# Even and odd tokens interleaved on the partitions of a sliding-attention transformer layer

## The chip, the cores and the metric

The kernel runs on one core of one Trainium2 chip. Its engines work side by side: TensorE (PE, with PEld for the loading of its weights), VectorE (DVE), ScalarE (ACT), GpSimd (POOL), and SyncE (SP), which here issues nearly all transfers between DRAM and SBUF. The metric is the time of one execution in microseconds (us), as the median of several runs.

## What is computed

One layer over 2048 tokens with 640 channels, all in fp32: LayerNorm, attention with 32 heads of 20 channels, output projection and residual, LayerNorm, a SwiGLU network of width 1728 and residual. Attention is local and dilated: a token looks at itself and at the seven tokens 2, 4, ..., 14 before it, so even tokens never see odd ones.

```
h  = x + attention(layernorm(x)) @ wo
h2 = h + (silu(n @ w_gate) * (n @ w_up)) @ w_down      with n = layernorm(h)

idx    = pos[:, None] - 2 * arange(8)[None, :]          # window 8, dilation 2
logits = einsum("bhsd,bhswd->bhsw", q, k[idx]) * 20**-0.5, -1e9 where idx < 0
o      = einsum("bhsw,bhswd->bhsd", softmax(logits), v[idx])
```

## The kernel before

**Tiles.** The tokens come in four blocks of 512: 128 partitions with four tokens each (j = 0 to 3). Partitions 0 to 63 hold the even tokens of a block, 64 to 127 the odd ones; x and the output lie in DRAM in that order. The heads come in four groups of 8, 160 channels each. fp32 products are made of two parts of every operand, a high and a low one, in three passes. ACT makes the high part (a cast), DVE the low one (a subtraction): L667 and L668 for the weights of Q, K and V, L598 and L599 for turned columns, L1040 (low part) for the activations of the SwiGLU network.

**Buffers.** `fa` is one wide SBUF buffer that holds many things in ranges of its columns: the x tiles of a block (XR), the normalized x (XN), weights as they land, constants. `kv` holds loaded K and V, `st` the projected Q, K and V on their way out, `pq` the operands of attention, `h` the residual rows, `sha` and `shb` the columns that PE multiplies.

**Stages of a block and a group of heads.** LayerNorm 1: statistics by DVE (L513 and L514, a pair of statistics and their aggregate for one tile) or by ACT (L491 to L503). Transposition into columns by PE (L641) or, for some blocks, by DVE and DRAM: one DVE transpose of the block (L602), four stores to `ysc` (L604), one load of the columns (L608), then split by L598 and L599. Projection by PE (L696), eviction by ACT into `st` (L703), stores of K and V into the DRAM scratch `ksc` and `vsc` (L716) and of Q into `qsc` (L726, L729, L732). Attention loads Q (L747) and the windows of K and V (L752): a partition gets its four tokens and the seven before them, 11 x 160 = 1760 columns, for even and odd tokens by one transfer each over 64 partitions. Rows before the first token are zeros, stored once by L460. DVE multiplies Q with the K window (L767), sums (L773), ACT takes the exponentials, DVE multiplies with the V window (L808), adds up (L817) and turns the result (L824), which is stored to `osc` (L830). Then the output projection (L901; for the last block L1238), LayerNorm 2, gate and up (L989) and down (L1004, and L1158 and L1405 for two blocks in another scheme), and the output stores (L1423, L1499).

**Order.** Every operation is registered with its engine and with the ranges of columns that it reads and writes. A table of numbers, `ORDER`, written into the kernel, gives the order in which the operations of all engines are emitted; each engine runs its own in that order. SP's queue is one such list. Each transfer takes one of eight DMA semaphores in turn, so a transfer waits until the one eight before it has landed. Waits between engines are made when the program is built, from the accesses of the instructions as they are emitted, not from the ranges that were registered.

Of the kernel before, what the change touches and what calls it, by code (L numbers as in the profile page):

```python
# [21 lines left out]
SEQ = S // 2 + W - 1  # L22
# [305 lines left out]
def program(tc, x_in, wqkv_in, wo_in, ffn_in, ffl_in, const_in, out):  # L328
# [8 lines left out]
    with tc.tile_pool(name="sb", bufs=1) as sb, tc.tile_pool(  # L337
# [1270 lines left out]
```

## Time and profile before

| | |
|---|---|
| time, median of 3 runs | 843.38 us (842.36, 844.35, 843.38) |
| time of the profiled execution | 845.17 us |
| its span, first to last instruction | 843.4 us |
| granted TensorE clock | 1.00 |
| PE busy | 835.2 us (99%), 4049 matmuls |
| DVE busy | 744.5 us (88%), 934 instructions |
| ACT busy | 426.3 us (51%), 774 instructions |
| DMA packets | 89877, 174.88 MB, mean 207 GB/s |

Busy shares are means over the whole span. For a single stage one reads the busy time in that stretch and what ended the idle time in it. In rows of the trace, the two numbers in front are start and length in us; brackets at the end give the idle time before and what ended it. SPq rows are the issues of transfers by SP, not the transfers themselves.

### The profile page before, as it was taken

The numbers are of one execution on the slowest core, as the hardware profiler recorded it, in microseconds if no ns is written. First come the engines' busy times: TensorE is split into PE (matmuls) and PEld (weight loads), VectorE is DVE, ScalarE is ACT, GpSimd is POOL, SyncE is SP. The second block draws the span as 40 slices with busy tenths as digits, with TensorE's granted clock in tenths as the row PEclk, the third lists the DMA queues.
The fourth block names the chain that finished last, engine by engine and source line by source line (L and its number), as shares of the span: only waits on it lengthen the run. The fifth ranks groups of instructions, "written<-read, shape, count | busy, mean of one in ns | idle before, by whom it ended". The sixth has DMA issues, their size and how long they took to land. (4 is left out here: it accounts for less than half of the span.)

```text
span 843.4 us, 11052 instructions
## 1 busy us (share of the span) xinstructions
PE 835.2 (99%) x4049; PEld 717.4 (85%) x4049; DVE 744.5 (88%) x934; ACT 426.3 (51%) x774; POOL 3.4 (0%) x14
## 2 busy tenths in 40 slices
PE   8999999999999999999999999999999999999998
PEld 7888888889888888888888888888888888888998
DVE  6599999999999999999999999996797676576996
ACT  7966476244873343567345347554464323335451
POOL 0000000000000000000000000000000000000000
PEclk9999999999999999999999999999999999999999
DMA  7988977678788898877999989977522133475002
GB/s 250 261 214 239 271 177 195 186 209 234 175 246 250 270 272 289 229 237 234 299 288 304 261 242 270 257 281 274 167 78 100 57 113 100 156 256 222 0 33 93
DMA packets 89877, 174.88 MB, mean 207 GB/s; under 512 B 33744, under 2 KB 53200, under 8 KB 89056
## 3 DMA queue, kind: packets, MB, share of 16 engines
q1 hardware_dynamic: 88416, 173.53, 67.7%
q10 hardware_dynamic: 1408, 0.66, 0.3%
q8 instruction: 31, 0.51, 0.2%
q14 instruction: 22, 0.18, 0.1%
HBM read 126.04 MB, written 46.80 MB: 205 GB/s over the span
## 5 line engine op out<-in xcount | busy, mean ns | idle before, releaser
L989 PE MATMUL bank<-shb,rb 128*128 128x512 f32 x930 | 227.0, 390 | 1.4 <-DVE fa L1028 0.7
L989 PEld LDWEIGHTS bank<-shb,rb 128*128 128x128 f32 x930 | 173.2, 188 | 38.4 <-DVE fa L1028 2.1
L1004 PE MATMUL bank<-rb,acts 128*128 128x512 f32 x464 | 121.4, 391 | 0.0
L1004 PEld LDWEIGHTS bank<-rb,acts 128*128 128x128 f32 x464 | 86.4, 188 | 17.3
L767 DVE TENSOR_TENSOR pq<-kv,pq 128x2560 f32<-128x2560 f32 x32 | 90.2, 2819 | 3.2 <-DMA pq<-qsc 1.9
L817 DVE TENSOR_TENSOR pq<-pq 128x1280 f32<-128x1280 f32 (+2 forms) x96 | 89.6, 934 | 2.2
L808 DVE TENSOR_TENSOR pq<-kv,pq 128x2560 f32<-128x2560 f32 x32 | 90.3, 2821 | 1.3 <-DMA kv<-vsc 0.7
L773 DVE TENSOR_REDUCE pq<-pq 128x128 f32<-128x2560 f32 x32 | 90.1, 2814 | 0.2
L703 ACT ACTIVATE st<-bank,fa 128x480 f32<-128x480 f32 (+3 forms) x120 | 50.4, 475 | 43.2 <-PE bank L696 40.8
L901 PE MATMUL bank<-ra 128*128 128x320 f32 x360 | 55.9, 309 | 0.9 <-ACT fa L904 0.9
L901 PEld LDWEIGHTS bank<-ra 128*128 128x128 f32 x360 | 54.2, 188 | 2.7 <-ACT fa L904 1.3
L970 ACT CAST rb<-fa 128x1280 fp32r<-128x1280 f32 (+1 forms) x35 | 42.5, 1217 | 25.2 <-DMA fa<-in_ffn_dram 20.0
L696 PE MATMUL bank<-ra,sha 128*128 128x480 f32 (+2 forms) x240 | 53.6, 380 | 0.0
L696 PE MATMUL bank<-rb,sha 128*128 128x512 f32 (+1 forms) x240 | 52.6, 378 | 0.0
L696 PE MATMUL bank<-ra,shb 128*128 128x512 f32 (+1 forms) x240 | 52.0, 378 | 0.0
L696 PE MATMUL bank<-rb,shb 128*128 128x512 f32 (+1 forms) x230 | 50.8, 379 | 0.0
L696 PEld LDWEIGHTS bank<-ra,shb 128*128 128x128 f32 x240 | 45.0, 188 | 6.5
L696 PEld LDWEIGHTS bank<-rb,sha 128*128 128x128 f32 x240 | 44.9, 188 | 6.4
L696 PEld LDWEIGHTS bank<-ra,sha 128*128 128x128 f32 x240 | 44.5, 188 | 6.6 <-ACT sha L643 0.2
L696 PEld LDWEIGHTS bank<-rb,shb 128*128 128x128 f32 x230 | 42.9, 188 | 6.3
L965 DVE TENSOR_TENSOR rb<-fa,rb 128x640 fp32r<-128x640 f32 (+1 forms) x54 | 43.4, 818 | 1.3 <-DMA lsc<-rb 0.7
L1027 ACT ACTIVATE fa<-bank 128x512 f32<-128x512 f32 x34 | 20.3, 598 | 42.4 <-PE bank L989 38.4
(211 smaller groups left out, 1264.8 us busy)
## 6 DMA issues: line engine op xcount, KB each, us to landing
fa<-in_ffn_dram SPq DMA_DIRECT2D x35, 960.0 KB, 7.1
kv<-ksc SPq DMA_DIRECT2D x32, 440.0 KB, 6.7
kv<-vsc SPq DMA_DIRECT2D x32, 440.0 KB, 7.4
rb<-lsc SPq DMA_DIRECT2D x17, 640.0 KB, 5.8
lsc<-rb SPq DMA_DIRECT2D x13, 640.0 KB, 6.0
rb<-lsc SPq DMA_DIRECT2D x19, 320.0 KB, 6.8
ksc<-st SPq DMA_DIRECT2D x32, 160.0 KB, 3.7
vsc<-st SPq DMA_DIRECT2D x32, 160.0 KB, 3.1
```

Source lines behind the costliest of these rows:

```text
L696: T.matmul(banks[bk][:, 0:n], l, r_(wq(g, w, c) + shift, n), start=(p, c) == first_mm, stop=(p, c) == last_mm)
L703: P.add("ACT", act(m) + 0.06, lambda: A.activation(stage_t()[:, o : o + NJ * m].rearrange("p (t j c) -> p t j c", j=NJ, c=w)[:, :, j, :], ...
L767: P.add("DVE", dve(2560), lambda: V.tensor_tensor(pq(PROD, 2560).rearrange("p (j w c) -> p j w c", j=2, w=W), window(ko, 2 * jp), pq(qo + ...
L773: P.add("DVE", dve(2560), lambda: V.tensor_reduce(logits(lo)[:, :, 16 * jp : 16 * jp + 16].rearrange("p h n -> p n h"), pq(PROD, 2560).rea ...
L808: V.tensor_tensor(pq(PROD, 2560).rearrange("p (j n d) -> p j n d", j=2, d=DH), bass.AP(tensor=v.tensor, offset=v.offset, ap=[list(v.ap[0]) ...
L817: V.tensor_add(dst(v), v[:, :, 0:m, :], v[:, :, m : 2 * m, :])
L901: T.matmul(banks[bk][:, 0:320], l, r_(m, 320), start=p == 0 and c == 0, stop=p == 2 and c == NC - 1)
L965: low(640, lambda E, o=o: E.tensor_sub(ws(t, lo + o, 640)[p0:], fa[p0:, raw + o : raw + o + 640], ws(t, hi + o, 640)[p0:].bitcast(F32)), [ ...
L970: P.add("ACT", act(n), lambda: A.copy(ws(wt, gu, n), f(raw, n)), r=[rf(raw, n)], w=[rws(wt, gu, n)], prio=PR["fh"])
L989: T.matmul(banks[bk], ws(wt, gu + 1280 * w + wid * c + col, 128), x(a, c), start=p == 0 and c == 0, stop=p == 2 and c == NC - 1)
L1004: T.matmul(banks[k], l, m, start=first and p == 0, stop=stop and p == len(passes) - 1)
L1027: P.add("ACT", act(512), lambda: A.activation(f(so, 512), banks[5], AF.Silu), r=[pb(5)], w=[rf(so, 512)], prio=0, table="silu")
```

## The change

Partition p now holds a token of parity p mod 2: even and odd tokens alternate. A token's window then lies in its own partition and in the two of the same parity below it, two and four partitions away. The scratch of K and V is laid out by row of eight tokens, parity and 640 columns, so that one transfer of 128 partitions stores a block's K (or V), and two transfers over all 128 partitions load a window: one of 480 columns (three tokens of halo, L759) and one of 2 x 640 columns (the four tokens before and the partition's own four, L755). x and the output keep their order in DRAM, so each of their transfers is now two, one for the even and one for the odd partitions (`get`, L444, and `give`, L448). The zeros before the first token are four small transfers for K and four for V, and the constants for the mask come in two halves. The instructions of PE and DVE are the same in kind, shape and number; ACT has three table loads fewer. SP issues 550 transfers, not 543. The table `ORDER` is a new one of the same kind; the beginning of a row of each stands in the diff.

```diff
-SEQ = S // 2 + W - 1
+ROWS = S // 8 + 2
 ORDER = (
-    (3, 1, 1), (3, 0, 1), (2, 0, 1), (0, 0, 1), (1, 0, 1), (4, 2, 1), (4, 7, 1), ...
+    (3, 1, 1), (4, 2, 1), (3, 0, 1), (2, 0, 1), (2, 7, 1), (4, 7, 1), (1, 0, 1), ...
...
-        ksc = dr.tile([NG, 2, SEQ, GC], F32, name="ksc")
+        ksc = dr.tile([NG, ROWS, 2, NJ * GC], F32, name="ksc")
...
+        def get(t, o, n, x):
+            for a in range(2):
+                Q.dma_start(t[a:128:2, o : o + n], x[64 * a : 64 * a + 64])
+        def give(x, t, o, n):
+            for a in range(2):
+                Q.dma_start(x[64 * a : 64 * a + 64], t[a:128:2, o : o + n])
...
         def zero_halo(t):
-            Q.dma_start(
-                t[:, :, 0 : W - 1, :].rearrange("g a r c -> (g a) (r c)"),
-                pq_t()[0 : NG * 2, PROD : PROD + 1120],
+            for a in range(2):
+                Q.dma_start(t[:, 0, a, GC:], pq_t()[0:NG, PROD : PROD + 480])
+                Q.dma_start(t[:, 1, a, :], pq_t()[0:NG, PROD : PROD + 640])
...
         def load_x(b, js=None):
             if b:
-                ... Q.dma_start(f(XR, 2560), x_in[b].rearrange("p j c -> p (j c)")) ...
+                ... get(fa, XR, 2560, x_in[b].rearrange("p j c -> p (j c)")) ...
             for j in js:
-                ... Q.dma_start(f(XR + 640 * j, 640), x_in[0, :, j, :]) ...
+                ... get(fa, XR + 640 * j, 640, x_in[0, :, j, :]) ...
...
-            def put(par, dst, o):
+            def put(dst, o):
                 Q.dma_start(
-                    dst[g, par, 7 + 256 * b : 7 + 256 * b + 256, :].rearrange("(r j) c -> r (j c)", j=NJ),
-                    stage_t()[64 * par : 64 * par + 64, o : o + 640],
+                    dst[g, 64 * b + 2 : 64 * b + 66].rearrange("r a c -> (r a) c"),
+                    stage_t()[:, o : o + 640],
...
                     def ld(dst=dst, o=o, par=par):
-                        a = dst[g, par, 256 * b, :]
-                        Q.dma_start(kv_t()[64 * par : 64 * par + 64, o : o + 1760],
-                                    bass.AP(tensor=a.tensor, offset=a.offset, ap=[[640, 64], [1, 1760]]))
+                        if par:
+                            a = dst[g, 64 * b + 1, 0, :]
+                            Q.dma_start(kv_t()[:, o + 480 : o + 1760].rearrange("p (k c) -> p k c", k=2),
+                                        bass.AP(tensor=a.tensor, offset=a.offset, ap=[[640, 128], [1280, 2], [1, 640]]))
+                        else:
+                            a = dst[g, 64 * b, 0, GC:]
+                            Q.dma_start(kv_t()[:, o : o + 480], bass.AP(tensor=a.tensor, offset=a.offset, ap=[[640, 128], [1, 480]]))
...
-                P.add("SP", 0.45, lambda: Q.dma_start(out[2 + b, :, j, o : o + c], h_t()[:, lo : lo + c]), ...
+                P.add("SP", 0.9, lambda: give(out[2 + b, :, j, o : o + c], h_t(), lo, c), ...
```

What the table and the new transfers make of the order shows at three places. In the rows below, the first name is the line of the kernel, then the operation, the buffer written and read, the shape written, and what the instruction waits for: an engine or one of the eight DMA semaphores. Lines of the changed kernel are 3 to 6 higher than those of the kernel before.

*The start up to the first attention product, SP and ACT.* SP before:

```order
L587 DMA fa<-in_x_dram 128x640 x3
L660 DMA fa<-in_wqkv_dram 128x480 x3
L587 DMA fa<-in_x_dram 128x640
L660 DMA fa<-in_wqkv_dram 128x480
L1522 DMA fa<-in_const_dram 128x32 [waits DMAHW0_49]
```

SP of the change:

```order
L444 DMA fa<-in_x_dram 64x640 x2
L444 DMA fa<-in_x_dram 64x640 [waits DVE_49]
L444 DMA fa<-in_x_dram 64x640 x3
L663 DMA fa<-in_wqkv_dram 128x480 x2
L663 DMA fa<-in_wqkv_dram 128x480 [waits DMAHW0_49]
L663 DMA fa<-in_wqkv_dram 128x960 [waits DMAHW1_49]
```

The third transfer of x, which is the first half of the second tile, has a wait on VectorE that no transfer there had before, and the weights stand behind six transfers of x, not three.

Further on, Q, K and V of the first block are evicted by ACT (L703 before, L706 now) from four banks; `rb` is where weights of the next group go. ACT before:

```order
L703 ACTIVATE st<-bank_72,fa 128x3x160 [waits DVE_49,PE_49]
L703 ACTIVATE st<-bank_71,fa 128x3x160 [waits PE_49]
L703 ACTIVATE st<-bank_70,fa 128x3x160 [waits PE_49]
L703 ACTIVATE st<-bank_73,fa 128x3x160 [waits PE_49]
L491 ACTIVATE fa<-fa 128x640 [waits DMAHW5_49,DMAHW0_49]
```

ACT of the change:

```order
L706 ACTIVATE st<-bank_71,fa 128x3x160 [waits DVE_49,PE_49]
L670 CAST rb<-fa 128x512 [waits DMAHW1_49,DMAHW0_49]
L536 ACTIVATE fa<-fa 128x2 [waits Activation_49]
L670 CAST rb<-fa 128x512
L670 CAST rb<-fa 128x512 [waits DMAHW3_49,DMAHW2_49]
L670 CAST rb<-fa 128x512
L706 ACTIVATE st<-bank_70,fa 128x3x160 [waits PE_49]
L706 ACTIVATE st<-bank_72,fa 128x3x160 [waits DVE_49,PE_49]
L706 ACTIVATE st<-bank_73,fa 128x3x160 [waits PE_49]
```

SP of the change, behind the last of these evictions:

```order
L719 DMA ksc<-st 128x640 [waits DMAHW5_49,Activation_49]
L465 DMA ksc<-pq 4x480 [waits DMAHW6_49]
L466 DMA ksc<-pq 4x640 [waits DMAHW7_49]
L465 DMA ksc<-pq 4x480 [waits DMAHW0_49]
L466 DMA ksc<-pq 4x640 [waits DMAHW1_49]
L663 DMA fa<-in_wqkv_dram 128x2x448 [waits DMAHW2_49,DVE_49]
L731 DMA qsc<-st 128x640 [waits DMAHW3_49]
L719 DMA vsc<-st 128x640 [waits DMAHW4_49]
L759 DMA kv<-ksc 128x480 [waits DMAHW6_49,DMAHW5_49,DMAHW7_49,DMAHW1_49,DMAHW0_49]
L755 DMA kv<-ksc 128x2x640
L749 DMA pq<-qsc 128x640 [waits DMAHW3_49]
```

Four casts moved in between the evictions, and the zero transfers for K stand between the store of K and its load.

*The turned columns of the second block, SP and DVE.* SP before, from the load of the columns to that of the next block's x:

```order
L608 DMA fa<-ysc 128x5x512 [waits DMAHW6_49,DMAHW1_49,PE_49]
L729 DMA qsc<-st 128x640 [waits DMAHW7_49]
L830 DMA osc<-pq 32x5x64 [waits DMAHW0_49]
L732 DMA qsc<-st 512x1x32 [waits Activation_49]
L716 DMA ksc<-st 64x640 [waits DMAHW2_49,Activation_49]
L830 DMA osc<-pq 32x5x64 [waits DMAHW3_49,DVE_49]
L584 DMA fa<-in_x_dram 128x2560 [waits DMAHW4_49]
```

SP of the change:

```order
L607 DMA ysc<-fa 32x20x128 [waits DMAHW6_49,DVE_49]
L607 DMA ysc<-fa 32x20x128 [waits DMAHW7_49]
L607 DMA ysc<-fa 32x20x128 [waits DMAHW0_49]
L607 DMA ysc<-fa 32x20x128 [waits DMAHW1_49]
L836 DMA osc<-pq 32x5x64 [waits DMAHW2_49]
L836 DMA osc<-pq 32x5x64 [waits DMAHW3_49]
L611 DMA fa<-ysc 128x5x512 [waits DMAHW4_49,DMAHW6_49,DMAHW1_49,DMAHW7_49,DMAHW0_49,PE_49]
L444 DMA fa<-in_x_dram 64x2560 [waits DMAHW5_49,Activation_49]
L444 DMA fa<-in_x_dram 64x2560
```

DVE of the change, from the second V product after the transpose on:

```order
L814 TENSOR_TENSOR pq<-kv,pq 128x2560 [waits DVE_49]
L823 TENSOR_TENSOR pq<-pq 128x2x640 [waits DVE_49]
L823 TENSOR_TENSOR pq<-pq 128x2x320 [waits DVE_49]
L823 TENSOR_TENSOR pq<-pq 128x2x160 [waits DVE_49]
L830 STREAM_TRANSPOSE pq<-pq 128x2x5x32 [waits DMAHW5_49,DMAHW3_49,DVE_49]
L602 TENSOR_TENSOR sha<-fa,sha 128x4x128 [waits DMAHW5_49,DMAHW4_49,DMAHW6_49,PE_49,Activation_49]
L602 TENSOR_TENSOR sha<-fa,sha 128x4x128
```

The load of x moved up to stand right behind that of the columns and waits for ACT; the first subtraction of the columns (L602 now, L599 before) waits for three DMA semaphores, where it waited for one.

*PE around 559 us.* `bank7` takes the output projection of the last block (L1238 before, L1244 now), `acts` is the split activation. Before:

```order
L1238 MATMUL bank7_77<-ra_66 128x320 [waits DVE_49]
L1238 MATMUL bank7_77<-ra_66 128x320 x3
L1004 MATMUL bank3_73<-rb_67,acts_2094 128x512 x3
L1004 MATMUL bank4_74<-acts_2094,rb_67 128x512 x3
L1004 MATMUL bank2_72<-rb_67,acts_2094 128x512 x3
L1004 MATMUL bank4_74<-acts_2094,rb_67 128x512 [waits DVE_49]
```

Of the change:

```order
L1244 MATMUL bank7_77<-ra_66 128x320 x9
L1010 MATMUL bank3_73<-rb_67,acts_2076 128x512 x3
L1010 MATMUL bank1_71<-rb_67,acts_2076 128x512 x3
L1010 MATMUL bank4_74<-acts_2076,rb_67 128x512 x3
L1010 MATMUL bank0_70<-rb_67,acts_2076 128x512 x3
L1244 MATMUL bank7_77<-ra_66 128x320 [waits Activation_49]
L1244 MATMUL bank7_77<-ra_66 128x320 x8
L1010 MATMUL bank4_74<-acts_2076,rb_67 128x512 [waits DVE_49]
```

Nine more products of the output projection stand ahead of the wait for VectorE.

More of the change, by code (lines that the diff above doesn't have):

```diff
@@ L394, in program @@
         banks = [psp.tile([128, 512], F32, name=f"bank{i}") for i in range(8)]
-        ksc = dr.tile([NG, 2, SEQ, GC], F32, name="ksc")
-        vsc = dr.tile([NG, 2, SEQ, GC], F32, name="vsc")
+        ksc = dr.tile([NG, ROWS, 2, NJ * GC], F32, name="ksc")
+        vsc = dr.tile([NG, ROWS, 2, NJ * GC], F32, name="vsc")
         qsc = dr.tile([NB, NG, 128, NJ, GC], F32, name="qsc")
@@ L459, in zero_halo @@
         def zero_halo(t):
-            Q.dma_start(
-                t[:, :, 0 : W - 1, :].rearrange("g a r c -> (g a) (r c)"),
-                pq_t()[0 : NG * 2, PROD : PROD + 1120],
-            )
+            for a in range(2):
+                Q.dma_start(t[:, 0, a, GC:], pq_t()[0:NG, PROD : PROD + 480])
+                Q.dma_start(t[:, 1, a, :], pq_t()[0:NG, PROD : PROD + 640])
         for nm, t in (("K", ksc), ("V", vsc)):
@@ L583, in load_x @@
             if b:
-                P.add("SP", 0.65, lambda: Q.dma_start(f(XR, 2560), x_in[b].rearrange("p j c -> p (j c)")), w=[rf(XR, 2560)], prio=PR["x"], nbytes=nb(512, 2560))
+                P.add("SP", 1.0, lambda: get(fa, XR, 2560, x_in[b].rearrange("p j c -> p (j c)")), w=[rf(XR, 2560)], prio=PR["x"], nbytes=nb(512, 2560))
                 return
             for j in js:
-                P.add("SP", 0.45, lambda j=j: Q.dma_start(f(XR + 640 * j, 640), x_in[0, :, j, :]), w=[rf(XR + 640 * j, 640)], prio=0, nbytes=(1.3 if j else 1.1) * nb(128, 2560))
+                P.add("SP", 0.9, lambda j=j: get(fa, XR + 640 * j, 640, x_in[0, :, j, :]), w=[rf(XR + 640 * j, 640)], prio=0, nbytes=(1.3 if j else 1.1) * nb(128, 2560))
         def span(nm, lo, hi):
@@ L721, in qkv @@
             for nmd, dst, o in (("K", ksc, ko), ("V", vsc, ko + 640)):
-                for par in range(2):
-                    P.add("SP", 0.65, lambda par=par, dst=dst, o=o: put(par, dst, o), r=[("ab", o, o + 640)],
-                          w=[(f"{nmd}{g}{par}", 1000 + 256 * b, 1256 + 256 * b)], prio=PR["kvs"], nbytes=nb(64, 2560))
+                P.add("SP", 0.65, lambda dst=dst, o=o: put(dst, o), r=[("ab", o, o + 640)],
+                      w=[(f"{nmd}{g}{par}", 1000 + 256 * b, 1256 + 256 * b) for par in range(2)], prio=PR["kvs"], nbytes=nb(128, 2560))
                 if nmd == "K" and n == 448:
@@ L750, in ld @@
                     def ld(dst=dst, o=o, par=par):
-                        a = dst[g, par, 256 * b, :]
-                        Q.dma_start(kv_t()[64 * par : 64 * par + 64, o : o + 1760],
-                                    bass.AP(tensor=a.tensor, offset=a.offset, ap=[[640, 64], [1, 1760]]))
+                        if par:
[5 more added lines that the diff above has]
+                            Q.dma_start(kv_t()[:, o : o + 480], bass.AP(tensor=a.tensor, offset=a.offset, ap=[[640, 128], [1, 480]]))
                     lo_r = 0 if b == 0 else 1000 + 256 * (b - 1)
-                    P.add("SP", 0.45, ld, r=[(f"{nmd}{g}{par}", lo_r, 1000 + 256 * (b + 1))], w=[(f"fakv{par}", o, o + 1760)], prio=PR["atl"], nbytes=nb(64, 7040))
+                    P.add("SP", 0.45, ld, r=[(f"{nmd}{g}{q}", lo_r, 1000 + 256 * (b + 1)) for q in range(2)], w=[(f"fakv{par}", o, o + 1760)], prio=PR["atl"], nbytes=nb(128, 5120 if par else 1920))
             return b, g, n, ko, vo, qo, lo, mo
@@ L874, in wo @@
             if b:
-                P.add("SP", 0.6, lambda: Q.dma_start(h_t()[:, h0 : h0 + 2560], x_in[b].rearrange("p j c -> p (j c)")),
+                P.add("SP", 1.0, lambda: get(h_t(), h0, 2560, x_in[b].rearrange("p j c -> p (j c)")),
                       w=[("sha", h0, h0 + 2560)], prio=PR["old"], nbytes=nb(512, 2560))
@@ L910, in wo @@
                     xr = XR + 640 * (j % 2)
-                    P.add("SP", 0.45, lambda j=j, xr=xr: Q.dma_start(f(xr, 640), x_in[0, :, j, :]), w=[rf(xr, 640)], prio=PR["old"], nbytes=nb(128, 2560))
+                    P.add("SP", 0.9, lambda j=j, xr=xr: get(fa, xr, 640, x_in[0, :, j, :]), w=[rf(xr, 640)], prio=PR["old"], nbytes=nb(128, 2560))
                     P.add("DVE", dve(640), lambda lo=lo, hi=hi, j=j, xr=xr: V.tensor_add(h_t()[:, lo:hi], f(xr, 640), f(XN + 640 * j, 640)),
@@ L1212, in wo3 @@
             hr = lambda j, o=0, n=640: ("sha", 2560 + 640 * j + o, 2560 + 640 * j + o + n)
-            P.add("SP", 0.6, lambda: Q.dma_start(h_t()[:, 2560:5120], x_in[3].rearrange("p j c -> p (j c)")), w=[("sha", 2560, 5120)], prio=PR["old"], nbytes=nb(512, 2560))
+            P.add("SP", 1.0, lambda: get(h_t(), 2560, 2560, x_in[3].rearrange("p j c -> p (j c)")), w=[("sha", 2560, 5120)], prio=PR["old"], nbytes=nb(512, 2560))
             slot = lambda i: OT + 512 * i
@@ L1422, in store @@
                 lo = 2560 * b + 640 * j + o
-                P.add("SP", 0.45, lambda: Q.dma_start(out[2 + b, :, j, o : o + c], h_t()[:, lo : lo + c]), r=[("sha", lo, lo + c)], prio=3, nbytes=nb(128, 4 * c))
+                P.add("SP", 0.9, lambda: give(out[2 + b, :, j, o : o + c], h_t(), lo, c), r=[("sha", lo, lo + c)], prio=3, nbytes=nb(128, 4 * c))
             ps = range(m)
@@ L1498, in finish @@
                     lo, hi = hsl(b, j, o, e - o)
-                    P.add("SP", 0.45, lambda lo=lo, hi=hi, o=o, e=e, j=j: Q.dma_start(out[b, :, j, o:e], h_t()[:, lo:hi]), r=[("sha", lo, hi)], prio=3, nbytes=nb(128, 4 * (e - o)))
+                    P.add("SP", 0.9, lambda lo=lo, hi=hi, o=o, e=e, j=j: give(out[b, :, j, o:e], h_t(), lo, hi - lo), r=[("sha", lo, hi)], prio=3, nbytes=nb(128, 4 * (e - o)))
         def ln2_columns(b, prio):
@@ L1521, in program, with load_mask @@
         load_x(0, (3,))
-        P.add("SP", 0.45, lambda: Q.dma_start(f(MASK, 32), const_in[:, 0:32]), w=[rf(MASK, 32)], prio=6, nbytes=nb(128, 128))
+        def load_mask():
+            for a in range(2):
+                Q.dma_start(fa[a:128:2, MASK : MASK + 32], const_in[64 * a : 64 * a + 64, 0:32])
+        P.add("SP", 0.9, load_mask, w=[rf(MASK, 32)], prio=6, nbytes=nb(128, 128))
         ln1(0)
```

454 rows, old and new, of the table ORDER are left out of this document.

## The prediction

> **What bounds the kernel now.** I read the busy times first, then the waits of TensorE (PE), then busy time by stretch, then the groups of VectorE (DVE).
>
> The first line is part 1 of the page, the rest the waits of PE, with us in total, times, and the longest.
>
> ```profile
> PE 835.2 (99%) x4049; PEld 717.4 (85%) x4049; DVE 744.5 (88%) x934; ACT 426.3 (51%) x774; POOL 3.4 (0%) x14
> ```
> ```profile
> PE bank L568 <- POOL rb L1508: 1.9, 1, 1.9
> ...
> PE bank L1004 <- DVE acts L1040: 0.3, 1, 0.3
> ```
>
> PE looks like the whole story: busy for 99%, hardly a wait. But busy time is a mean over stages, so I cut the span at the first attention product (36.19) and at PE's last wait before a stretch without any (559.21). Columns: PE, PEld, DVE, ACT, POOL busy with counts, granted clock, DMA share, GB/s.
>
> ```profile
> 0.00:36.19 36.19, 33.83 (x154) 28.57 (x155) 18.73 (x45) 28.60 (x64) 1.17 (x7) 1.00 0.83 252
> 36.19:559.21 523.02, 520.40 (x2499) 446.17 (x2497) 511.30 (x518) 282.08 (x511) 0.73 (x2) 1.00 0.84 246
> 559.21:840.17 280.96, 280.96 (x1398) 242.62 (x1398) 214.02 (x372) 115.63 (x200) 1.51 (x5) 1.00 0.37 131
> ```
>
> In the middle DVE is busy for 511.30 of 523.02 us; what is left is 11.7 us over 518 instructions, 23 ns apiece, the step from one to the next. PE is as full only because the order gives it exactly what DVE releases. At 559.21 PE waits for a DVE subtraction (L1040), and everything DVE did is a queue ahead of that point. After it PE has 280.96 us without a gap, and DVE has slack (214.02). So the time is made of four parts: DVE's idle time in the head (36.19 − 18.73 = 17.46, a little of it steps), DVE's work up to L1040, PE's rest (280.96), and the tail, 843.4 − 840.17 = 3.2. DVE's and PE's instructions are the same in kind, shape and number after the change. So I look for idle time added to or taken from DVE before 559, PE work moved across that wait, and the tail.
>
> The groups of DVE that read K and V, with shapes kept apart: busy, mean ns of one | idle before them and what ended it. The last row has three shapes in one: a half, a quarter and an eighth of a product's columns.
>
> ```profile
> L808 DVE TENSOR_TENSOR pq<-kv,pq 128x2560 f32<-128x2560 f32 x32 | 90.3, 2821 | 1.3 <-DMA kv<-vsc 0.7
> L767 DVE TENSOR_TENSOR pq<-kv,pq 128x2560 f32<-128x2560 f32 x32 | 90.2, 2819 | 3.2 <-DMA pq<-qsc 1.9 <-DMA kv<-ksc 0.8 <-DMA osc<-pq 0.2
> L773 DVE TENSOR_REDUCE pq<-pq 128x128 f32<-128x2560 f32 x32 | 90.1, 2814 | 0.2
> ...
> L824 DVE STREAM_TRANSPOSE pq<-pq 128x320 f32<-128x320 f32 x32 | 16.3, 510 | 0.8
> ```
> ```profile
> L817 DVE TENSOR_TENSOR pq<-pq 128x1280 f32<-128x1280 f32 (+2 forms) x96 | 89.6, 934 | 2.2
> ```
>
> **The change part by part.** *K and V in one store and two full-width loads.* DMA issues: KB each, median us to landing.
>
> ```profile
> kv<-ksc SPq DMA_DIRECT2D x32, 440.0 KB, 6.7
> kv<-vsc SPq DMA_DIRECT2D x32, 440.0 KB, 7.4
> rb<-lsc SPq DMA_DIRECT2D x17, 640.0 KB, 5.8
> ```
>
> A load of 440 KB over 64 partitions takes 6.7 to 7.4, one of 640 KB over 128 takes 5.8, so the new loads should land earlier. But in all 64 products DVE waited 0.8 + 0.7 = 1.5 us for K and V: that is the most this can bring. It can bring nothing (the waits come from when a buffer comes free, not from the transfer). I take −0.5, as the loads are wider but their order behind other transfers is new.
>
> The Trainium skill ("SBUF — State Buffer", section "Door 1: The DMA port swizzle") says that partitions 0 to 63 reach 8 of 16 ports and all 128 reach 16. The three rows agree in direction (6.7 for fewer bytes, 5.8 for more). By that rule alone the whole 1.5 would go; the sum would be 1.0 lower.
>
> *x in halves, at the start.* The start of the trace of before:
>
> ```profile
> 0.80 1.35 SPq L587 DMA_DIRECT2D fa<-in_x_dram  x3
> 2.19 1.38 SPq L660 DMA_DIRECT2D fa<-in_wqkv_dram  x3
> 3.59 0.89 DVE L513 BATCH_NORM_STATS2 fa<-fa 128x6 f32<-128x320 f32 x2 [2.66 <-DMA fa<-in_x_dram]
> 3.61 0.43 SPq L587 DMA_DIRECT2D fa<-in_x_dram  x1
> ...
> 4.51 0.21 DVE L514 BATCH_NORM_AGGREGATE fa<-fa 128x2 f32<-128x12 f32 x1
> ...
> 6.88 0.89 DVE L513 BATCH_NORM_STATS2 fa<-fa 128x6 f32<-128x320 f32 x2 [1.57 <-DMA fa<-in_x_dram]
> ...
> 9.66 3.30 PE L696 MATMUL bank<-ra,sha 128*128 128x480 f32 x14
> ```
>
> Before, three x tiles go out between 0.80 and 2.15 and nothing holds them. In the order of the changed kernel the third transfer (first half of the second tile) waits for VectorE. Counting DVE's instructions, that is the aggregate of the first tile's statistics, ready at 4.51 + 0.21 = 4.7. It does not need those columns; the wait is made for a transfer that steps over every second partition of the same buffer. So four halves at 0.43 to 0.45 each leave from 4.7 to 6.5, and all that is queued behind them on SP is late: the weights at 6.5, not 2.19. The tile that was there at 6.88 has its second half asked for at 6.1; with some 2.5 to land (the three first tiles were there 3.59 − 0.80 = 2.8 after the first issue) it is there at 8.7, and the first projection, 9.66 − 6.88 = 2.8 behind it, starts at 11.5: **1.8 late**.
>
> The way from there to the first attention product:
>
> ```profile
> 23.29 1.22 ACT L703 ACTIVATE st<-bank,fa 128x480 f32<-128x480 f32 x2 [1.07 <-PE bank L696]
> ...
> 24.54 1.17 SPq L716 DMA_DIRECT2D ksc<-st  x2
> ...
> 26.87 0.69 DVE L668 TENSOR_TENSOR rb<-fa,rb 128x512 fp32r<-128x512 f32 x1 [4.34 <-DMA ksc<-st]
> ...
> 27.04 0.58 SPq L729 DMA_DIRECT2D qsc<-st  x1
> ...
> 30.13 0.33 SPq L747 DMA_DIRECT2D pq<-qsc  x1
> ...
> 36.19 2.83 DVE L767 TENSOR_TENSOR pq<-kv,pq 128x2560 f32<-128x2560 f32 x1 [1.86 <-DMA pq<-qsc]
> ```
> ```profile
> L667 ACT CAST rb<-fa 128x512 fp32r<-128x512 f32 x5 | 3.0, 614 | 0.0
> ```
> ```profile
> L668 DVE TENSOR_TENSOR rb<-fa,rb 128x448 fp32r<-128x448 f32 x5 | 2.9, 617 | 0.0
> ```
>
> ScalarE now has four casts of 0.614 (2.5 us) ahead of the last three evictions, so K is stored some 3.6 later (1.8, and 1.8 of the casts; the rest passes while PE ends). That is 28.2. Behind it on SP stand four small zero transfers and one of weights, ahead of the store of q: five issues at 0.33 to 0.45, 2.0 us, where before the second K store and two V stores stood, about 1.9. So the round trip of q keeps its length (24.54 to 36.19, 11.65) and the first product comes at 39.8, 3.6 late. DVE does three more 448-column subtractions first, 3 × 0.617 = 1.85 at most, 1.6 by the distance of their starts. So DVE's idle time grows by **+2.0**. From below: without the late start and the casts showing, the product comes at 36.2 with 1.6 more work done, −1.6. From above: +5, if the weights land late as well.
>
> *x of block 1 beside the turned columns.* Some LayerNorm output is turned by DVE, stored, loaded as columns, then split by ACT (L598) and DVE (L599).
>
> ```profile
> 72.50 2.85 DVE L602 STREAM_TRANSPOSE fa<-fa 128x2560 f32<-128x2560 f32 x1
> ...
> 88.13 0.39 SPq L608 DMA_DIRECT2D fa<-ysc  x1
> ...
> 96.06 0.62 ACT L598 CAST sha<-fa 128x512 fp32r<-128x512 f32 x1 [4.66 <-DMA fa<-ysc]
> ...
> 96.67 0.43 SPq L584 DMA_DIRECT2D fa<-in_x_dram  x1
> ...
> 101.96 0.68 DVE L599 TENSOR_TENSOR sha<-fa,sha 128x512 fp32r<-128x512 f32 x1
> ```
>
> Issues: all of the execution, then the one at 96.67 alone (last row):
>
> ```profile
> fa<-in_x_dram SPq DMA_DIRECT2D x3, 1280.0 KB, 9.5
> ...
> ysc<-fa SPq DMA_DIRECT2D x4, 320.0 KB, 5.1
> fa<-ysc SPq DMA_DIRECT2D x1, 1280.0 KB, 7.9
> ```
> ```profile
> fa<-in_x_dram SPq DMA_DIRECT2D x1, 1280.0 KB, 5.7
> ```
>
> Before, x of the next block is loaded after the columns, and neither engine waits for it. In the changed order its two halves stand right behind the load of the columns. The first waits for ACT's first cast, and the second cast and the first subtraction wait for both halves to land, again over other columns of the same buffer. Count from the end of the transpose. DVE then has to the subtraction one L773 (2.82), one L779 (2.81), two L814 with three sums and a transpose each (2 × (2.82 + 2.80 + 0.51) = 12.3), those groups being L767, L773, L808, L817 and L824 before, and eight small ones (1.8, estimate): 19.7. The columns take four stores in a row (four issues at 0.58, as the store of q above, and 5.1 to land: 7.4), the load 7.9, the cast 0.62, two halves (0.9 and 5.7): 22.5 (7.4 + 7.9 + 0.6 + 6.6). **+2.7** of DVE idle. From below 0 (the stores land sooner); from above 6.5, with 9.5 for x, the median of such loads, in place of 5.7.
>
> *Order at 559.* Nine 320-wide products of Wo that stood behind PE's wait for L1040 now stand ahead of it, and DVE's work ahead of L1040 is the same. The chain of waits has their price:
>
> ```profile
> 559.21 2.35 PE bank L1004 x9
> ...
> 561.99 1.31 PE bank L1238 x9
> ```
>
> PE's rest after the wait shrinks by **−1.3**. It brings nothing if the wait is no longer the one that decides.
>
> *Out in halves.* The last rows go out by two issues: one more at 0.43, less what a half lands sooner: **+0.35** (0 to 0.43). The x loads of the later blocks and the halo cost issues on SP alone; the cover is the distance at which they are asked for. ACT's three fewer table loads fall where it has 282.08 busy of 523.02: nothing.
>
> The Trainium skill ("DMA: Bandwidth & Descriptors", section "Rules for kernel authors") says not to split a transfer into two halves of the partitions, since both halves run on the same DMA engines and serialize. By that rule no half lands sooner than the whole, and the tail costs the full 0.43 in place of 0.35; no run here shows a split load of x yet.
>
> Sum: +2.0 + 2.7 − 0.5 − 1.3 + 0.35 = **+3.2**. The profiled execution took 845.17, 1.8 over its span and 1.8 over the median; it becomes 848.4. Against the median of 843.38 that is 846.6; I say **846.7**, with 844.5 to 849.5 as this case's own range.
>
> **The rivals.**
>
> A, *the head gains* (faster). The new order does three more subtractions ahead of the first product. If that product comes at about 36.2 to 36.5, DVE's idle time falls by 1.6. With columns in time that is −1.6 + 0 − 0.5 − 1.3 + 0.35 = −3.05: **840.3**. It decides when the first attention product starts before 37.8 (36.19 + 1.6): from there the head is a gain. For it: before, DVE stands 4.34 us in the head ahead of a subtraction of weights (the row at 26.87), which earlier weights would end sooner, and x tiles asked for in halves may land sooner. Against it: the wait at 4.7, and casts ahead of evictions.
>
> B, *late but covered* (within 0.2%). Head +2.0, columns in time: +0.55, **843.9**. For it: stores of 320 KB that follow each other may land sooner than 5.1, which was measured with others between them; 2.7 is small against a path of 22.5.
>
> C, *x in traffic*. The x load takes 9.5 beside K and V loads, and SP, which waits for the cast meanwhile, issues those late: +7.0, **850.4**. Two of three such loads were slower than the 5.7 one.
>
> **How the numbers follow.** Forecast 0.48, A 0.20, B 0.20, C 0.12. About 0.2% (1.7 us) is what a measurement of this kernel can tell from no change: faster is below 841.7, slower above 845.1. Faster: A nearly whole and a little of B, 0.21. Within: most of B, the low end of the forecast, 0.23. Slower: 0.56. The range takes in A and C: 840.5 to 850.5.
>
> **What would show it.** Right: the third x transfer issued at about 4.7, the first projection at 11 to 12, the first attention product at 39 to 41; near 105 a DVE wait of 1 to 5 us that ends with x, and an ACT cast that ends with x too; nine 320-wide products ahead of the last wait for L1046 (L1040 before). Wrong: a first product before 37.8, no DVE wait for x near 105, or PE with gaps that DVE does not explain; then my count of what the transfers wait for is off, or the K and V loads gave more than the 1.5 they can.

## The result, and the profile after

The changed kernel takes **853.89 us** (852.99 to 854.86, four runs), the kernel before 843.15 beside it: 1.0126 times as long (95% interval 1.0109 to 1.0144). Measured once more beside the experiments the ratio was 1.0127 (1.0098 to 1.0155). The prediction had the sign, slower, but its 846.7 is 7 us too low and the time lies above its range. The medians of two kernels further down leave out one run each that took far longer than all others (1197.69 us of the changed kernel, 1931.37 us of the one with K and V in halves).

The profiled execution of the changed kernel took 852.99, its span is 851.3; before, 845.17 and 843.4. The first is the fastest run of the changed kernel, the second is above all three runs of the kernel before, so the profiles show 7.9 us of the 10.7 between the medians. Busy times of the changed kernel:

```profile
PE 835.4 (98%) x4049; PEld 718.0 (84%) x4049; DVE 743.5 (87%) x934; ACT 420.9 (49%) x771; POOL 3.4 (0%) x14
```

The work is the same as before (PE 835.2, DVE 744.5). The waits of PE, in us in total, times, longest:

```profile
PE bank L644 <- ACT fa L499: 3.6, 1, 3.6
PE bank L571 <- POOL rb L1514: 1.9, 1, 1.9
PE bank L699 <- ACT st L706: 1.3, 1, 1.3
PE bank L644 <- DVE fa L518: 1.1, 1, 1.1
PE bank L556 <- DVE shb L560: 1.1, 2, 0.8
```

Before, PE waited for DVE's low part of the activations (L1004) and for other results between 288 and 559 us. None of that is left. All waits now lie early, as the cut of the span shows: to the first projection (14.37), to the first attention product (42.48), to the last early wait, to the end of PE. Columns as in the prediction's table of stretches.

```profile
0.00:14.37 14.37, 7.74 (x26) 5.65 (x27) 4.54 (x12) 5.05 (x10) 1.17 (x7) 0.81 0.55 169
14.37:42.48 28.11, 28.11 (x130) 24.09 (x131) 15.91 (x37) 25.03 (x57) 0.00 (x0) 0.98 0.84 264
42.48:149.77 107.29, 104.93 (x502) 90.73 (x502) 100.42 (x91) 59.80 (x140) 0.00 (x0) 1.00 0.66 216
149.77:844.47 694.70, 694.63 (x3393) 597.54 (x3392) 622.10 (x796) 330.98 (x565) 2.23 (x7) 1.00 0.60 203
```

From 149.77 on PE is busy for 694.63 of 694.70 us: **PE is the bound now**, not DVE. At the place where PE waited for L1040 before (L1046 now), DVE's result is there at 563.80 and PE comes for it 1.2 us later:

```profile
563.11 0.69 DVE L1046 TENSOR_TENSOR acts<-fa,acts 64x512 fp32r<-64x512 f32 x1
...
565.01 0.63 PE L1010 MATMUL bank<-acts,rb 128*128 128x512 f32 x2
```

Where the 7.9 us are: PE's idle time was 2.36 before 36.19 and 2.62 from there to 559.21, 4.98 in all; it is 6.63 + 2.36 + 0.07 = 9.06 now, 4.1 more. PE's busy time is 0.2 more. And from PE's end to the span's end it was 843.4 − 840.17 = 3.2, and is 851.3 − 844.47 = 6.8, 3.6 more. So three places: the start, a stretch around 112 us, and the tail.

*The start*, from the trace of the changed kernel:

```profile
0.80 6.95 SPq L444 DMA_DIRECT2D fa<-in_x_dram  x6
...
4.20 0.89 DVE L516 BATCH_NORM_STATS2 fa<-fa 128x6 f32<-128x320 f32 x2 [3.27 <-DMA fa<-in_x_dram]
...
7.79 2.96 SPq L663 DMA_DIRECT2D fa<-in_wqkv_dram  x6
...
10.36 0.89 DVE L516 BATCH_NORM_STATS2 fa<-fa 128x6 f32<-128x320 f32 x2 [4.44 <-DMA fa<-in_x_dram]
...
13.73 0.59 ACT L670 CAST ra<-fa 128x480 fp32r<-128x480 f32 x1 [1.50 <-DMA fa<-in_wqkv_dram]
...
14.37 1.17 PE L699 MATMUL bank<-ra,sha 128*128 128x480 f32 x2
...
42.48 2.83 DVE L773 TENSOR_TENSOR pq<-kv,pq 128x2560 f32<-128x2560 f32 x1
```

The six halves are issued over 6.95 us, with the wait for DVE's aggregate inside; the weights leave at 7.79 (2.19 before), the tile that DVE reads next, the third one issued, is there at 10.36 (6.88). The first projection starts at 14.37 (9.66), 4.7 late, right behind the cast of weights that had to land first. The first attention product comes at 42.48, 6.3 late.

*Around 112 us*, the columns, the x load and the engines behind it:

```profile
103.71 0.62 ACT L601 CAST sha<-fa 128x512 fp32r<-128x512 f32 x1 [0.29 <-DMA fa<-ysc]
104.36 1.18 SPq L444 DMA_DIRECT2D fa<-in_x_dram  x2
...
112.00 0.62 ACT L601 CAST sha<-fa 128x512 fp32r<-128x512 f32 x1 [7.67 <-DMA fa<-in_x_dram]
...
112.66 1.29 DVE L602 TENSOR_TENSOR sha<-fa,sha 128x512 fp32r<-128x512 f32 x2 [3.96 <-ACT sha L601]
...
113.79 1.50 PE L699 MATMUL bank<-rb,shb 128*128 128x448 f32 x6 [1.27 <-ACT st L706]
```

The x load leaves after the first cast, and the second cast waits 7.67 us for it. DVE loses 3.96. And ACT, which stands in that wait, has evictions behind it, for which PE waits 1.27. Some 35 us later PE waits another 1.1 for DVE (L560).

*The tail*, SP's issues of the last output stores and the last additions that they wait for. Before:

```profile
834.13 6.93 SPq L1423 DMA_DIRECT2D out_dram<-h  x7
...
840.21 0.49 DVE L1418 TENSOR_TENSOR h<-bank,h 128x320 f32<-128x320 f32 x1 [0.83 <-PE bank L1405]
```

Now:

```profile
837.67 11.34 SPq L448 DMA_DIRECT2D out_dram<-h  x18
...
842.30 0.49 DVE L1424 TENSOR_TENSOR h<-bank,h 128x320 f32<-128x320 f32 x1 [0.83 <-PE bank L1411]
...
843.18 0.49 DVE L1424 TENSOR_TENSOR h<-bank,h 128x320 f32<-128x320 f32 x1 [0.39 <-PE bank L1411]
...
844.50 0.49 DVE L1424 TENSOR_TENSOR h<-bank,h 128x320 f32<-128x320 f32 x1 [0.83 <-PE bank L1411]
```

Eighteen halves in 11.34 us, 0.63 from one to the next, the last of them issued 4 us after the last result. Before, seven whole stores stood in 6.93 us, with SP waiting for results between them, and the last issue ended 0.4 us after the last result.

And K and V, the groups that read them:

```profile
L814 DVE TENSOR_TENSOR pq<-kv,pq 128x2560 f32<-128x2560 f32 x32 | 90.3, 2821 | 0.6
L773 DVE TENSOR_TENSOR pq<-kv,pq 128x2560 f32<-128x2560 f32 x32 | 90.2, 2818 | 0.5
```

No transfer stands behind the idle time any more. The 1.5 us of waits are gone, as the prediction allowed.

### The profile page after: what moved, and what is told of

The parts are those of the page before. It is cut to its first block, busy times and chain, and to the rows that moved or that the text cites. A ratio compares the mean times of both kernels' runs of the same rounds, so it can differ in the third digit from the quotient of the medians.

```text
span 851.3 us, 11043 instructions
## 1 busy us (share of the span) xinstructions
PE 835.4 (98%) x4049; PEld 718.0 (84%) x4049; DVE 743.5 (87%) x934; ACT 420.9 (49%) x771; POOL 3.4 (0%) x14
## 4 chain that ended last, share of the span: by engine, by line
PE 88%; DVE 4%; DMA 3%; ACT 2%; SPq 1%; issue 1%; DVEq 0%; ACTq 0%
PE bank L995 29%; PE bank L699 16%; PE bank L1010 15%; PE bank L1164 13%; PE bank L907 6%; PE bank L1411 6%; PE bank L1244 2%; DMA fa<-in_x_dram 1%; DVE pq L773 1%; PE bank L556 1%; DMA fa<-ysc 1%; DVE pq L823 1%; DVE pq L814 1%; DMA ysc<-fa 1%; DMA fa<-in_wqkv_dram 1%
## 5 line engine op out<-in xcount | busy, mean ns | idle before, releaser
L706 ACT ACTIVATE st<-bank,fa 128x480 f32<-128x480 f32 (+3 forms) x120 | 50.7, 474 | 50.0 <-PE bank L699 48.6
L1024 ACT CAST acts<-fa 128x512 fp32r<-128x512 f32 x36 | 22.3, 621 | 42.1 <-DVE fa L1034 39.6
```

The costliest lines, as they stand in the source:

```text
L706: P.add("ACT", act(m) + 0.06, lambda: A.activation(stage_t()[:, o : o + NJ * m].rearrange("p (t j c) -> p t j c", j=NJ, c=w)[:, :, j, :], ...
```

## The experiments

Two theories. **Theory 1**: the halves of x and of the output cost the time, by waits that come with them and by their issues; K, V and the new order do no harm. **Theory 2**: the new order, or K and V in wide transfers, costs it. Most kernels below keep x and the output in DRAM in the interleaved order, so that each transfer can be whole or in halves while the table of the order stays the changed one:

```diff
-    x = a(A_x.reshape(NB, 64, NJ, 2, D).transpose(0, 3, 1, 2, 4).reshape(NB, 128, NJ, D))
+    x = a(A_x.reshape(NB, 64, NJ, 2, D).transpose(0, 1, 3, 2, 4).reshape(NB, 128, NJ, D))
...
-                Q.dma_start(t[a:128:2, o : o + n], x[64 * a : 64 * a + 64])
+                Q.dma_start(t[a:128:2, o : o + n], x[a:128:2])
```

Ratios are to the kernel before on the same chip. Ratios of four or five runs are known to about 0.15 to 0.3%, so the parts are also read from the profiles.

**Everything whole.** All x, output and mask transfers over 128 partitions.

```diff
-                P.add("SP", 0.9, lambda j=j: get(fa, XR + 640 * j, 640, x_in[0, :, j, :]), ...
+                P.add("SP", 0.9, lambda j=j: Q.dma_start(f(XR + 640 * j, 640), x_in[0, :, j, :]), ...
...
-                P.add("SP", 0.9, lambda: give(out[2 + b, :, j, o : o + c], h_t(), lo, c), ...
+                P.add("SP", 0.9, lambda: Q.dma_start(out[2 + b, :, j, o : o + c], h_t()[:, lo : lo + c]), ...
```

The other uses of `get` and `give`, and the mask, are changed in the same way.

> The changed kernel with x and the output kept in DRAM in the interleaved order, so that every transfer of x, of the output and of the mask is one over 128 partitions. K and V, and the table of the order, are as changed. Theory 1 (the loss comes from waits that the transfers over every second partition bring, plus slow output issues): first projection near 10 us, no wait for x near 112, tail 3.2 us; the 5.3 us at the start, 3.1 us between 112 and 149 and 3.6 us in the tail come back: about 842. Theory 2 (the loss is the new order and K and V in wide transfers): it stays above 850.

Measured: 840.84, ratio 0.9979 (0.9965 to 0.9993). Theory 2 falls: with the same order and the same K and V, the kernel is 0.2% faster than the one before. Measured again with the kernels compared further down:

> The kernel with everything whole once more. If its gain is real: 0.2% below the kernel before again, 0.9965 to 0.9993. If the first measurement was luck: within 0.1% of it.

840.53, ratio 0.9964 (0.9949 to 0.9979). Its waits of PE:

```profile
PE bank L571 <- POOL rb L1514: 1.9, 1, 1.9
PE bank L995 <- ACT fa L1033: 0.9, 2, 0.6
PE bank L644 <- DVE sha L647: 0.3, 1, 0.3
```

3.1 us, against 4.98 us of idle time before. No kernel of the study is faster. Its first attention product shows what the new order does without the halves:

```profile
38.11 2.81 DVE L773 TENSOR_TENSOR pq<-kv,pq 128x2560 f32<-128x2560 f32 x1
```

That is 1.9 later than before (36.19), and DVE is idle for 17.85 us up to there (17.46 before). The other 4.4 of the 6.3 come with the halves.

**One place at a time.** The output stores whole (the second edit above, at both uses of `give`), the start whole (the four x tiles of the first block), the x loads of the later blocks whole (those for LayerNorm 1):

> The changed kernel with DRAM in the interleaved order, x still in halves over every second partition, only the output stores whole. Both theories: nothing but the tail moves; if the tail of 6.9 us is the queue of output issues on SP (18 at 0.63 us), it falls to about 3.3 and the time to about 850.3. If the tail is the landing of the last rows, it stays at 853.9.

> The changed kernel with only the four x tiles of the first block whole, the rest in halves. Theory 1: first projection near 10 us, 4 us earlier; TensorE keeps its clock there; TensorE is the bound from 149 us on, so most of 5.3 us comes back unless VectorE takes over: 848 to 850. If the start is covered later by other slack: no change, 853.9.

> The changed kernel with DRAM in the interleaved order and only the x loads of blocks 1 to 3 for LayerNorm 1 whole, the start and the output in halves. Theory (TensorE is the bound from about 149 us on, so each loss before that counts in full): no wait for x near 112, the 3.1 us between 112 and 149 come back, 853.9 - 3.1 = 850.8. Rival (VectorE is the bound further on and is late from the start anyway): less than 1 us comes back.

Measured: output whole 850.46, ratio 1.0103 (1.0087 to 1.0118). Start whole 846.95, ratio 1.0061 (1.0046 to 1.0076). Later blocks whole 851.43, ratio 1.0112 (1.0097 to 1.0128). Against 1.0126 these are 0.23, 0.65 and 0.14% of 843, 1.9, 5.5 and 1.2 us. They add up to 8.6 of the 12.4 us between the changed kernel and everything whole. What is missing is about the size of the intervals, so the sum does not tell whether a fourth place matters (the x loads for the residual and the mask stay in halves in all three). The DRAM order alone does not move the start: with the output whole and x in halves the first projection comes at 14.26, as in the changed kernel.

In the profiles each does what it should. Output whole, the last issues of SP:

```profile
837.96 7.69 SPq L1429 DMA_DIRECT2D out_dram<-h  x9
...
844.80 0.49 DVE L1424 TENSOR_TENSOR h<-bank,h 128x320 f32<-128x320 f32 x1 [0.83 <-PE bank L1411]
```

The last store leaves right behind the last addition; the span ends at 848.2, 2.9 us behind it, where the changed kernel needs 6.3 (851.3 − 844.99). Start whole:

```profile
0.80 1.34 SPq L590 DMA_DIRECT2D fa<-in_x_dram  x3
2.18 2.98 SPq L663 DMA_DIRECT2D fa<-in_wqkv_dram  x6
...
8.86 2.40 PE L699 MATMUL bank<-ra,sha 128*128 128x480 f32 x10
```

The first projection at 8.86, 5.5 us earlier than in halves. And later blocks whole:

```profile
104.55 1.14 ACT L601 CAST sha<-fa 128x512 fp32r<-128x512 f32 x2 [0.40 <-DMA fa<-ysc]
...
109.27 1.25 DVE L602 TENSOR_TENSOR sha<-fa,sha 128x512 fp32r<-128x512 f32 x2
```

The casts follow each other and DVE does not wait: the wait at 112 belongs to the strided halves, not to the order, in which the load of x stands where it stood.

**The tail alone, on one chip.** All loads of x whole, the output alone in halves, beside the changed kernel and everything whole:

> The changed kernel itself once more, beside the two kernels that follow, so that the parts are compared on one chip. All theories: 1.2 to 1.3% over the kernel before.

> The changed kernel with DRAM in the interleaved order, all loads of x and the mask whole, the output alone in halves. If the tail is the queue of 0.6 us issues: TensorE's part is that of the kernel with everything whole, the tail 6.9 in place of 3.4 us, so 3.4 us (0.4%) above that kernel, about 0.2% over the kernel before. If most of the loss sat in the output stores: near the changed kernel.

Measured on the same chip: changed 853.82, x whole 843.90 (ratio 1.0010, 0.9996 to 1.0025), everything whole 840.53. So of 13.3 us the x loads hold **9.9** and the output stores **3.4**, as expected. In the kernel with x whole the tail is again a row of halves, 18 issues in 11.33 us:

```profile
828.55 11.33 SPq L448 DMA_DIRECT2D out_dram<-h  x18
```

**Is it the wait, or the number of transfers?** The 5.5 us of the start can come from the wait for DVE inside SP's queue or from six issues in place of three. Two kernels take this wait of SP away and leave the six issues. In the first the halves are partitions 0 to 63 and 64 to 127:

```diff
-                Q.dma_start(t[a:128:2, o : o + n], x[a:128:2])
+                Q.dma_start(t[64 * a : 64 * a + 64, o : o + n], x[64 * a : 64 * a + 64])
...
-                Q.dma_start(x[a:128:2], t[a:128:2, o : o + n])
+                Q.dma_start(x[64 * a : 64 * a + 64], t[64 * a : 64 * a + 64, o : o + n])
```

> The changed kernel with x and the output in two transfers each, but of partitions 0 to 63 and 64 to 127 in place of every second one. Theory 1a (the waits cost it): the start and the stretch at 112 come back, only the tail stays: 853.9 - 5.3 - 3.1 = 845.5. Theory 1b (the number of transfers and their slower issue cost it): the start stays late by most of its 5 us, 850 or more.

In the second the first three x tiles are emitted ahead of all else (the table of the order begins with them, nothing else moves). The wait then falls on DVE:

```diff
 ORDER = (
-    (3, 1, 1), (4, 2, 1), (3, 0, 1), (2, 0, 1), (2, 7, 1), (4, 7, 1), ...
+    (4, 2, 1), (4, 7, 1), (4, 4, 1), (3, 1, 1), (3, 0, 1), (2, 0, 1), (2, 7, 1), ...
```

> The changed kernel with DRAM in the interleaved order, all in halves, and the first three x tiles emitted ahead of the first statistics, SP's own order as it is. So SP no longer waits for VectorE after the second half; the wait turns up on VectorE, whose first aggregate now waits for all six halves. If SP's wait is what makes the start late: the weights leave at 4.6 us, not 7.8, TensorE's first projections come 2 to 2.5 us sooner, 1.3% over the kernel before falls to 1.0%. If only the number and the price of the halves count: no change at all.

Measured: halves of neighbours 852.75, ratio 1.0116 (1.0087 to 1.0146); issued first 850.46, ratio 1.0084 (1.0056 to 1.0111), 3.4 us below the 853.82 of the changed kernel on the same chip. The starts of the two, neighbours first:

```profile
0.80 3.79 SPq L444 DMA_DIRECT2D fa<-in_x_dram  x6
...
4.62 2.96 SPq L663 DMA_DIRECT2D fa<-in_wqkv_dram  x6
...
11.24 1.22 PE L699 MATMUL bank<-ra,sha 128*128 128x480 f32 x3 [0.84 <-ACT ra L670]
```
```profile
4.62 2.96 SPq L663 DMA_DIRECT2D fa<-in_wqkv_dram  x6
...
7.48 0.21 DVE L517 BATCH_NORM_AGGREGATE fa<-fa 128x2 f32<-128x12 f32 x1 [2.46 <-DMA fa<-in_x_dram]
...
11.68 0.77 PE L699 MATMUL bank<-ra,sha 128*128 128x480 f32 x1
```

Without the wait the weights leave at 4.62 in both, and the first projection comes at 11.24 and 11.68, not at 14.37. With whole tiles it is 8.86. So of the 5.5 us by which the first projection is late, about **2.7 to 3.1 are the wait** and **2.4 to 2.8 the halves themselves**: six issues take 3.8 us where three take 1.34, and weights queue behind them. In all four kernels the first projection starts 6.6 to 7.1 us after the first weights leave (at 2.18, 4.62, 4.62 and 7.79). The upper 2.8 is not the halves alone: in the second kernel the false wait has only moved (DVE's aggregate waits 2.46 for tiles that it does not read). My expectation for the neighbours, 845.5, was wrong. In its profile the wait at 112 is gone, as expected, but other waits come in its place, the largest behind a load of attention results that took 13.26 us (467.49 to 480.75):

```profile
PE bank L907 <- ACT fa L910: 4.2, 1, 4.2
```

Whether loads over 64 neighbouring partitions hold up what is behind them, or whether that one load was late by chance, is open: one profile doesn't tell, and this kernel's runs spread widely (849.94 to 855.56).

**The clock.** In the start of the changed kernel the granted clock falls. In stretches of 5 us (columns as above):

```profile
5.00:10.00 5.00, 1.97 (x10) 1.20 (x8) 0.84 (x3) 1.36 (x4) 0.00 (x0) 0.88 0.58 169
10.00:15.00 5.00, 3.28 (x12) 2.52 (x13) 3.46 (x8) 2.84 (x6) 0.00 (x0) 0.50 0.89 301
```

To see whether that costs time of its own, 14 more warming matmuls were put where PE waits 3.6 us:

```diff
-                    warm(1, 512, [("b5", 0, 0.25)])
+                    warm(15, 512, [("b5", 0, 0.25)])
```

> The changed kernel with DRAM in the interleaved order, halves as they are, and 14 more warming matmuls (3.2 us, their result is not used) in the 3.6 us in which TensorE waits for the second x tile. If the fall of the granted clock to 0.5 between 10 and 15 us costs time of its own: the clock stays near 1, the transposes at 12 us and the first projections run at full pace, 1.0 to 1.6 us come back, about 852.5. If the late x and weights alone set the start: no change, 853.9.

Measured: 855.08, ratio 1.0154 (1.0139 to 1.0170), not faster than the changed kernel. The stretch from 10 to 15 now has a clock of 0.96, but the first projection starts at 14.77, since it waits for the cast of late weights, and behind that wait the clock falls after all:

```profile
14.77 1.17 PE L699 MATMUL bank<-ra,sha 128*128 128x480 f32 x2 [2.02 <-ACT ra L670]
```
```profile
15.00:20.00 5.00, 5.00 (x17) 4.26 (x18) 4.82 (x9) 4.59 (x12) 0.00 (x0) 0.70 0.64 214
```

From 15 to 20 the clock is 0.70 here and 0.94 in the changed kernel. So the fall was moved, not taken away, and this kernel does not show what it costs. That the slow clock did not set the first projection is seen in the changed kernel itself: the cast that it needs ends at 14.32, and it starts at 14.37. Behind it the clock is still 0.50 up to 15 and 0.70 from 15 to 16, which makes about 0.6 us of PE's work (an estimate: 0.63 × 0.50 + 1.00 × 0.30). What else made the kernel with more warming slower is open.

**The nine products.** Everything whole, and the nine products of Wo behind the wait again, as before the change (PE's instructions in their order, not code):

```diff
 L1010 MATMUL bank_70<-rb,acts 128x512 x3
-L1244 MATMUL bank_77<-ra 128x320 x9
 L1010 MATMUL bank_74<-acts,rb 128x512 x2
 L1010 MATMUL bank_72<-rb,acts 128x512 x2
 L1010 MATMUL bank_73<-rb,acts 128x512 x2
+L1244 MATMUL bank_77<-ra 128x320 x9
```

> The kernel with everything whole (840.84) with nine of the 320-wide output projection matmuls put back behind TensorE's wait for the low part near 557 us, as they stood before the change. If VectorE sets the time of that wait, as the prediction had it: TensorE waits 1.3 us longer there and the time is 842.2. If TensorE is the bound there in this kernel, its wait being 0.2 us: between 840.8 and 842.2, at least no more than 0.5 us slower.

Measured: 841.07, ratio 0.9980 (0.9968 to 0.9991), against 0.9979 with them ahead. No difference. PE around the place:

```profile
554.58 0.72 PE L1010 MATMUL bank<-acts,rb 128*128 128x512 f32 x2
555.15 1.09 PE L1010 MATMUL bank<-rb,acts 128*128 128x512 f32 x4
556.07 1.49 PE L1244 MATMUL bank<-ra 128*128 128x320 f32 x9
```

PE runs through without a listed wait, its matmul that waits for DVE among them (at 554.58; DVE's subtraction ends at 554.53). The 1.3 us of the prediction do not exist in this kernel.

**The width of K and V.** Everything whole, but each load of K and V in two of 64 partitions:

```diff
-                            Q.dma_start(kv_t()[:, o : o + 480], bass.AP(tensor=a.tensor, offset=a.offset, ap=[[640, 128], [1, 480]]))
+                            for h in range(2):
+                                Q.dma_start(kv_t()[64 * h : 64 * h + 64, o : o + 480],
+                                            bass.AP(tensor=a.tensor, offset=a.offset + 40960 * h, ap=[[640, 64], [1, 480]]))
...
```

> The kernel with everything whole (840.84) with each load of K and V in two transfers of 64 partitions, 128 loads more. If the width of the K and V loads is worth something, waits of VectorE for K and V come back, up to the 1.5 us of the kernel before or more: 841.5 to 843. If these loads are hidden: 840.8, no waits for kv.

Measured: 842.62, ratio 1.0012 (1.0002 to 1.0022), against 0.9979 for everything whole: 2.8 us by the ratios. By the medians it is 1.6 us above the 841.07 of the kernel with the products put back, which ran on the same chip. But DVE waits only 0.4 us for V in its profile. PE's waits of the middle are for ACT and DVE:

```profile
PE bank L998 <- ACT fa L1036: 0.8, 2, 0.5
PE bank L998 <- DVE fa L1037: 0.6, 1, 0.6
```

So the split costs something, though not at the products that read K and V. Loads of 64 partitions and 64 more issues on SP (not 128, as the expectation has it) come together here, and which of them it is stays open.

## Why the prediction was wrong, point by point

- **What failed, in short.** The sum of +3.2 met 7.9 in the profiles and 10.7 between the medians. Two of its terms were mis-sized: the output in halves (+0.35, measured 3.4) and the late start (1.8, measured 4.4). A third, the order at 559 (−1.3), does not exist, since it rested on DVE setting the time there.
- **The frame: DVE's work up to 559 us, then PE's rest.** Its first part came out near, with luck. DVE's subtraction at the wait starts at 563.11 and started at 558.46, 4.65 earlier; the first three terms gave 4.2. But DVE lost 4.6 in the start and 3.96 at 112, not 2.0 and 2.7, and then won some back in waits that are gone, 1.5 of it for K and V. The step from there to PE's end failed. PE lost time of its own: its idle time up to 149.77 is 8.99, where it had 2.36, while the 2.62 us that it waited for DVE and others later are gone. It came to the place 1.2 us after DVE's result and runs from 149.77 to its end without a wait, so the loss is read from PE. Even before, this frame was one of two readings: PE was busy for 520.40 of the 523.02 us in the middle and waited about 1 us of them for DVE.
- **The start, +2.0.** Right in mechanism: the third transfer waits for DVE's first aggregate, weights queue behind it, casts stand ahead of evictions. The term was mis-sized. I had issues of 0.43 to 0.45 for halves and weights from 6.5; the halves took 0.63 each (3.78 for six without a wait), the first tile landed later and the aggregate with it, and the weights left at 7.79. The first projection came at 14.37, not 11.5, the first product at 42.48, not 39.8. DVE's idle time up to there is 42.48 − 4.54 − 15.91 = 22.0, 4.6 more than before. The part for the casts and the three subtractions was right: +1.8 and −1.6 stand against 1.9 and DVE idle 0.4 longer with everything whole. Of the late first projection about half was not the wait but twice the issues. One reading was wrong too: 2.8 after the first issue the first tile alone was there; the other two were read at 4.53 and 6.88, though they had been issued by 2.15.
- **x beside the columns, +2.7.** The best step. The place, the cast that waits, the subtraction that waits are as predicted; the halves landed 7.6 after the first issue (6.6 predicted) and DVE lost 3.96, inside the bounds of 0 to 6.5. What the sum left out is ACT: it stood 7.67 us in that wait with evictions behind it, and PE waited 1.27 for one of them and 1.1 more at 147. Whole transfers remove all of it.
- **K and V, −0.5.** The waits of 1.5 us went entirely, the upper bound. By the rule of the Trainium skill ("SBUF — State Buffer", section "Door 1: The DMA port swizzle"), that all 128 partitions reach twice the ports of the first 64, the whole of it was to go, and the trace agrees as far as no wait for K or V is left. That the ports did it is not shown; the test by halves does not separate width from number.
- **The order at 559, −1.3.** Wrong: the term rested on DVE setting that wait. With PE as the bound it is 0, as the kernel with the products put back shows (0.9980 against 0.9979). In the changed kernel PE comes 1.2 us after DVE's result; with the nine products, 1.31 us, behind the wait it would have come 0.1 us too early.
- **The output in halves, +0.35.** Wrong by ten times: 3.4 us. I counted one more issue at the end. But the stores are a queue: the last results come 0.9 to 1.3 us apart (842.30, 843.18 and 844.50 in the rows of the tail), two issues take 1.26, so SP, already behind, never catches up and carries 4 us over the end.
- **A rule that spoke against the change.** The Trainium skill ("DMA: Bandwidth & Descriptors", section "Rules for kernel authors") advises one transfer over 128 partitions in place of two halves. I gave it 0.08 us. The runs agree with the advice: about 2.4 us in the start without any wait, 3.4 in the tail. The reason that the traces show is another than the one given there, that both halves run on the same DMA engines: here SP's queue is longer, 0.63 us for each half where a whole tile took 0.45.
- **The rivals.** None held. A (the first product before 37.8) and B (the columns in time) fall by the rows at 42.48 and 112.00. C had the right place, but an x load of 9.5 us; it took 7.6. The time beyond 850.5 came from the start and the tail, in which no rival lay.

## What to carry to other kernels

Price a transfer that becomes two by its queue, not by its landing: multiply the issue by all that stands in a row at the start and at the end, where the queue itself is the critical path. Look in the order for waits that no data asks for; a transfer that steps over partitions can bring them on far columns, and changing the layout in DRAM, so that the transfer is whole again, took away the waits and the issues together (840.53 against 853.82). And when a loss is early, ask again which engine is the bound behind it, before the later terms are added.

## What the runs showed of the hardware

Issues on SP: a whole x tile of 128 x 640 took 0.45 us (three in 1.34), a half of 64 x 640 took 0.63 (six in 3.78), whether its partitions were every second one or neighbours, and a half output store 0.63 as well (18 in 11.34). The loads of K and V show the same: 0.60 at the median over 64 partitions (L756 of the kernel with K and V in halves), 0.43 and 0.46 over 128 (L755 of the changed kernel). Fewer partitions made the issue longer, not shorter.

In the changed kernel PE waited 3.58 us up to 10.55; from 10.5 to 15 us the granted clock was 0.50, from 15 to 16 it was 0.70 and from 16 on 1.00, with PE busy throughout from 14.37. The Trainium skill ("TensorE: Matmul & The Clock Gate", section "Why this matters for your kernels") warns of idle gaps of PE above about 3 us; this trace agrees. Two other runs show that no single gap of that length is needed: with halves of neighbours the clock was 0.50 from 12 to 15 us after PE had waited 0.50, 0.71, 0.80 and 0.84 between 5.8 and 11.24, and with more warming matmuls it was 0.70 on the mean from 15 to 20 after one wait of 2.02. What the fall cost in the end is not shown.
